# Decays over the whole unit, later weight loads, an apart first gate load and unit ends combined bank by bank, in a gated recurrence followed by an ELU MLP

## The chip, the cores and the metric

The kernel runs on one core of one Trainium2 chip. A core has five engines with a queue of their own each: TensorE (PE in the profile, with its weight loads as PEld), VectorE (DVE), ScalarE (ACT), GpSimd (POOL) and SyncE (SP), which here only starts DMA transfers. The metric is device time in microseconds (us). Nine runs of the kernel before gave a median of 586.71 us (585.16 to 588.66). The profile is one execution of its own: 586.64 us, of which the trace spans 584.9 us. PE, DVE, ACT and POOL each run their own list of instructions strictly in the order written, because the kernel turns the scheduler off.

## The reference

```python
batch, n_heads, seq, head_dim = (4, 8, 768, 48)
n_tokens, d_model, d_ff = (3072, 384, 2048)
...
    f = 1.0 / (1.0 + np.exp(-f_logit))
    for t in range(S):
        state = f[:, :, t, :, None] * state + np.einsum('bhd,bhe->bhde', k[:, :, t], v[:, :, t])
        y[:, :, t] = np.einsum('bhd,bhde->bhe', q[:, :, t], state)
...
    x = np.ascontiguousarray(attn_out.transpose(0, 2, 1, 3)).reshape(B * S, H * D)
    h = x @ w_in
    g = np.where(h > 0.0, h, alpha * (np.exp(np.minimum(h, 0.0)) - 1.0))
    return (g @ w_out).astype(np.float32)
```

Each of 32 heads carries a 48 by 48 state that decays per row with the gate f. The output x, 3072 tokens of 384 features, goes through a two-layer MLP with 2048 hidden units and ELU. q, k, v and f are float32, the two weights are float64 (eight bytes a number).

## The kernel before

**Units.** The tokens are cut into 12 units of 256 (`U`), three to a batch (`UPB`). Heads go in pairs `p` = 0 to 3 (`HP`): one head of a pair on partitions 0 to 47, the other on 64 to 111 (`HALF`), with padding rows between. A unit has four chunks of 64 tokens (`C`, `NC`).

**Attention of a unit.** `gates` (L556) turns f_logit into 1/f = 1 + exp(-x) on ACT (L563, L564). `decays` (L570) runs a cumulative product of 1/f along the tokens on DVE (L576), takes its reciprocal (L579), and scales k by the first (L580, POOL) and q by the second (L583). The product restarts at each chunk: POOL puts the first column of each chunk into the tile `restart` and zeros it in f (L566, L567), and the scan takes the maximum with `restart`. For pair 0 of unit 0 it restarts by being four scans of 64 columns instead. `watch` (L587) notes whether any product has passed `LIMIT` (the flag that sends the program to a slower general kernel). `transposed` (L593) transposes k on PE and copies it out on ACT (L602, tile `kn`); `advance` (L642) makes the states' increments; `step` (L606) runs the states from chunk to chunk on DVE: add (L613), times the chunk's decay (L616). `scores` (L619), `mask` (L635), `outputs` (L656) and `carried` (L675) give y. `carried` copies y into `xt` on ACT (L693, L695) and moves sixteen-row pieces of it with six small DMAs on SP (L699): piece i goes to column j = i mod 3, so that column j of `xt` is whole after pieces j and j + 3.

**MLP.** A step P is one unit m and one of eight blocks j of 256 hidden units. `up(P)` (L774) is 12 matmuls into `psH` (L780), with two passes on ACT (L785, L786); column kt of `xt` is used by the matmuls kt = 0, 1, 2 in turn. `elu(P)` (L789) finishes ELU on DVE (L792) and, for units from 2 on, makes four sums (L802). `down(P)` (L804) is 8 matmuls of 384 columns (L813, units 0 and 1) or, from unit 2 on, 7 products of half width with both weights and their combinations `combos` (L835, 14 matmuls), into four banks `pm[0]` to `pm[3]`; when a unit ends, ACT copies one half bank (L846) and five DVE additions (L845) make the output tile `o`, which four DMAs store (L854). Those of the last unit's second half go over ACT's queue, all others over SP's.

**Weights.** There are 16 items of 768 KB, half of them blocks of `w_in` (four DMAs each, L500 and L501), half of `w_out` (one DMA, L495). `fetch(n)` starts item n into one of seven slots of `area`. `split(n)` (DVE, L515, L519), `lower(n)` (ACT, L525) and `merge(n)` (DVE, L533) turn float64 into float32; `merge(n)` then starts `fetch(n + 7)` into the slot that it has emptied.

**Order.** The main loop runs T over two steps per P: `elu(P - 1)` and `up(P)` at even T, `down(P - 2)` at odd T. What else belongs to a step stands in `plan` under its T. `order` puts the first step of unit 1 (1, 0) at P = 6, T = 12. Before the loop the start runs unit 0's attention by hand (L886 to L926), with `warm(n)`, matmuls on the identity whose result is not used (L881). SP's queue before the loop holds, in this order: `load(0)` (f, k, q, v of unit 0; half of f, k and q on ACT's queue), `fetch(0)`, `load(1)`, `fetch(1)`, `fetch(7)` (from `merge(0)`), `fetch(2)` to `fetch(6)`. In the loop it goes on with `fetch(8)` to `fetch(11)`, `load(2)`, `fetch(12)`, `fetch(13)`, the six pieces of unit 1's `xt`, `fetch(14)`, `fetch(15)`, `load(3)`.

**Eight in flight.** The transfers of SP and ACT use eight completion semaphores in turn. So each issue waits until the transfer eight places before it has landed, whatever else it waits for.

Of the kernel before, what the change touches and what calls it, by code (L numbers as in the profile page):

```python
# [356 lines left out]
def fast(ctx: ExitStack, tc: tile.TileContext, q, k, v, f_logit, w_in, w_out, out, flag):  # L357
# [13 lines left out]

    nc = tc.nc
# [19 lines left out]
    LIMIT = 2.0**60  # L392
# [14 lines left out]
    def load(u, other=None):  # L407

        b, s0 = u // UPB, (u % UPB) * U
        for n in "fkq":  # L410
            for r in range(2):
                ((other or nc.sync) if r else nc.sync).dma_start(
                    out=qkf[u % NB][n][HALF[r]],
                    in_=src[n][b, r::2, :, s0 : s0 + U].rearrange("p d s -> d p s"),
                )
        nc.sync.dma_start(
            out=vs[u % NB][:, :, 0:DM], in_=v[b, s0 : s0 + U].rearrange("(c t) n -> t c n", t=W)
        )
# [13 lines left out]

    restart = cst.tile([128, HP, U], FP32, name="restart")
    nc.vector.memset(restart[:], 0.0)
    fine = cst.tile([128, HP, NC], FP32, name="fine")
# [120 lines left out]
    def gates(u, pieces=(2, 2)):  # L556

        f = qkf[u % NB]["f"]
        pts[u] = sb.tile([128, HP, U], FP32, tag="p", name=f"p{u}")
        p = 0  # L560
        for n in pieces:
            a = f[:, p : p + n]
            nc.scalar.activation(a, a, AF.Exp, scale=-1.0)  # L563
            nc.scalar.activation(a, a, AF.Copy, bias=1.0)  # L564
            if u or p:
                nc.gpsimd.tensor_copy(restart[:, p : p + n, ::C], a[:, :, ::C])  # L566
                nc.gpsimd.memset(a[:, :, ::C], 0.0)  # L567
            p += n

    def decays(u, p):  # L570
# [3 lines left out]
        for c in range(1 if u or p else NC):  # L574
            a = g if u or p else g[:, c * C : (c + 1) * C]
            nc.vector.tensor_tensor_scan(  # L576
                out=a, data0=a, data1=restart[:, p] if u or p else a, initial=1.0, op0=ALU.mult, op1=ALU.max
            )
# [8 lines left out]
    def watch(u):  # L587
        nc.vector.scalar_tensor_tensor(
            out=fine[:], in0=qkf[u % NB]["f"][:, :, C - 1 :: C], scalar=LIMIT, in1=fine[:],
            op0=ALU.is_le, op1=ALU.mult,  # L590
        )
# [14 lines left out]
    def step(u, c):  # L606
# [3 lines left out]
        now = pus[u][c % 2][:, c // 2]  # L610
        s = sb.tile([128, HP, D], FP32, tag="state", name=f"state{u}_{c}", bufs=5)
        if u % UPB or c:
            nc.vector.tensor_tensor(out=s[:], in0=now, in1=sts[u, c][:], op=ALU.add)  # L613
            now = s[:]
        decay = pts[u][:, :, (c + 1) * C - 1 : (c + 1) * C].broadcast_to([128, HP, D])
        nc.vector.tensor_tensor(out=s[:], in0=now, in1=decay, op=ALU.mult)  # L616
# [123 lines left out]
    plan, later = {}, {}  # L740

    def at_step(step, *todo):
        plan.setdefault(step, []).extend(todo)
# [60 lines left out]
    def down(P):  # L804
# [25 lines left out]
        for bank, half, x, y in (  # L830
            (0, 0, a[0][0], b[0][0]), (3, 0, a[0][1], b[1][0]), (0, 1, s[:, 1], c[1]),
            (1, 0, s[:, 0], c[0]), (1, 1, s[:, 2], c[2]), (2, 1, a[1][1], c[3]), (2, 0, s[:, 3], b[1][1]),
        ):
            first = j == 0 and (bank, half) in ((0, 0), (3, 0), (1, 0), (2, 1))
            nc.tensor.matmul(  # L835
                pm[bank][:, half * DH : (half + 1) * DH], lhsT=x, rhs=y,
                start=first, stop=(j == NP - 1), skip_group_check=True,
            )
        if j == NP - 1:
            p = [[pm[i][:, h * DH : (h + 1) * DH] for h in range(2)] for i in range(4)]  # L840
            o = sb.tile([128, 2, DM], FP32, tag="o", name=f"o{m}")
            u2 = sb.tile([128, DH], FP32, tag="u2", name=f"u2_{m}", bufs=1)
            u43 = sb.tile([128, 2, DH], FP32, tag="u43", name=f"u43_{m}", bufs=1)
            flat = o[:].rearrange("p t f -> p (t f)")
            add = lambda to, x, y: nc.vector.tensor_tensor(out=to, in0=x, in1=y, op=ALU.add)  # L845
            nc.scalar.copy(u2[:], p[0][0])  # L846
            add(flat[:, 0:DH], p[3][0], u2[:])
            add(u2[:], p[0][1], u2[:])
            add(u43[:], pm[1][:].rearrange("p (h f) -> p h f", h=2), u2[:].unsqueeze(1).broadcast_to([128, 2, DH]))
            add(flat[:, 3 * DH :], p[1][0], u43[:, 1])  # L850
            add(flat[:, DH : 3 * DH], pm[2][:], u43[:].rearrange("p h f -> p (h f)"))
            for t in range(2):
                for h in ((1, 0) if t else (0, 1)):
                    (nc.scalar if t and m == NU - 1 else nc.sync).dma_start(  # L854
                        out=out[m * U + t * 128 : m * U + (t + 1) * 128, h * DH : (h + 1) * DH],
                        in_=o[:, t, h * DH : (h + 1) * DH],
                    )
# [32 lines left out]
    fetch(1)  # L890
# [18 lines left out]
    for c in range(NC - 1):  # L909
# [3 lines left out]
        )  # L913

    if wide:
        nc.gpsimd.memset(area[:, 2:].bitcast(I32)[:, :, 0:1], 0)
    for n in range(2, AHEAD):
        fetch(n)
    split(1)
# [3 lines left out]
    lower(1)  # L923
    decays(1, 1)
    step(0, NC - 1)
    watch(0)  # L926
    blank(2, nc.gpsimd)
# [3 lines left out]
    attention(1, (), (2, 4, 5, 6, 7))  # L931
    for n in range(1, NFT):
        t = max(needs[n][0] - 2, 0)
        at_step(t, lambda n=n: merge(n))
        if n > 1:
            later.setdefault(max(t - 2, 0), []).append(n)
# [16 lines left out]
    for T in range(NU * NFT):  # L953
# [9 lines left out]
        for n in later.pop(T, ()):  # L963
            split(n)
            lower(n)
# [47 lines left out]
```

## Time and profile before

| what | value |
|---|---|
| median of 9 runs | 586.71 us |
| profiled execution, whole / span of its trace | 586.64 / 584.9 us |
| granted TensorE clock, mean | 0.992 of full |
| busy: PE, PEld, DVE, ACT, POOL | 566.8, 492.5, 398.2, 217.4, 78.9 us |
| moved by DMA in all | 50.81 MB |
| unit 0's first f load: issue, landing | 1.55 and 1.56, 4.0 and 4.3 us later |
| first ACT gate (L563) / first scan (L576) | 5.93 / 6.82 us |
| first issue of `load(1)` / of `fetch(1)` / of `fetch(7)` | 10.06 / 14.81 / 21.69 us |
| first psH matmul of P = 0 / P = 1 / P = 6 | 33.48 / 39.02 / 71.46 us |
| last psM matmul ends / last addition ends | 577.67 / 579.09 us |

A busy PE is one that has a matmul in its pipe; ends of matmuls are modelled. Busy times of the engines overlap and do not add up to the span. Times such as 71.46 us count from the span's start.

### The profile page before, as it was taken

Reading aid. Unit: us, or ns where it says so; the run is one execution under the profiler, and the core shown is the slowest. Engines: PE = TensorE matmul, PEld = TensorE weight load, DVE = VectorE, ACT = ScalarE, POOL = GpSimd, SP = SyncE. Lnnn points to the kernel's source line nnn. Section 1 sums busy time; section 2 is a strip of 40 time slices with the busy share of each in tenths; the row PEclk is TensorE's granted clock in tenths of the full one; section 3 lists DMA queues with packets and bytes.
Section 4 is the critical chain, followed back from the end, with each engine's and each line's share of the span. In section 5 each row is a group of like instructions: output and inputs, shape, how many; then the busy total and the mean of one; then the engine's idle time right before and its main releaser. Section 6 shows DMA issues by size and latency. Waiting matters only on the chain.

```text
span 584.9 us, 13417 instructions
## 1 busy us (share of the span) xinstructions
PE 566.8 (97%) x5596; PEld 492.5 (84%) x5596; DVE 398.2 (68%) x806; ACT 217.4 (37%) x357; POOL 78.9 (13%) x161
## 2 busy tenths in 40 slices
PE   7689999999999999999999999999999999999995
PEld 3467777777899999999999899899899999999994
DVE  7799667666586676576676776766766767665852
ACT  3367845433433332432423333243252252232221
POOL 6350021020020020020021011011011011000000
PEclk9889999999999999999999999999999999999999
DMA  8999880061071061052053043033024010305401
GB/s 183 239 235 270 184 196 0 2 124 47 2 156 40 3 126 69 4 93 88 19 85 92 21 83 91 27 66 105 29 52 118 29 54 10 136 17 208 136 3 33
DMA packets 34823, 50.81 MB, mean 87 GB/s; under 512 B 4000, under 2 KB 27584, under 8 KB 34752
## 3 DMA queue, kind: packets, MB, share of 16 engines
q1 hardware_dynamic: 33840, 49.07, 34.1%
q8 instruction: 46, 0.75, 0.6%
q10 hardware_dynamic: 912, 0.79, 0.6%
q14 instruction: 25, 0.20, 0.1%
HBM read 44.04 MB, written 4.72 MB: 83 GB/s over the span
## 4 chain that ended last, share of the span: by engine, by line
PE 92%; DMA 3%; ACT 1%; DVE 1%; POOL 1%; issue 0%; SPq 0%; DVEq 0%; POOLq 0%; ACTq 0%
PE psH L780 43%; PE psM L835 31%; PE psM L813 7%; PE psS L629 2%; PE psY L666 2%; PE psU_a L650 2%; PE psY L686 2%; PE psT L598 2%; DMA q<-in_q_dram 1%; DMA area<-in_moe_w_in_dram 1%; DMA f<-in_f_logit_dram 1%; PE psW L881 1%; ACT f L564 0%; ACT f L563 0%; ACT area L525 0%
## 5 line engine op out<-in xcount | busy, mean ns | idle before, releaser
L780 PE MATMUL psH<-xt,wi 128*128 128x256 f32 x1152 | 268.6, 383 | 0.0
L780 PEld LDWEIGHTS psH<-xt,wi 128*128 128x128 f32 x1152 | 213.7, 190 | 30.4 <-issue 0.5
L785 ACT ACTIVATE gg<-psH 128x512 f32<-128x512 f32 x96 | 57.3, 597 | 267.5 <-PE psH L780 267.3
L792 DVE SCALAR_TENSOR_TENSOR gg<-gg,psH 128x512 f32<-128x512 f32 x96 | 65.8, 685 | 109.0 <-ACT gg L786 109.0
L835 PE MATMUL psM<-area,sums 128*128 128x192 f32 x480 | 91.1, 326 | 0.0
L579 DVE RECIPROCAL p<-f 128x256 f32<-128x256 f32 x48 | 84.1, 1753 | 1.7
L835 PEld LDWEIGHTS psM<-area,sums 128*128 128x128 f32 x480 | 80.2, 190 | 0.0
L835 PE MATMUL psM<-wo,gg 128*128 128x192 f32 x320 | 65.2, 326 | 0.0
L786 ACT ACTIVATE gg<-gg 128x512 f32<-128x512 f32 x96 | 60.5, 630 | 3.0
L835 PEld LDWEIGHTS psM<-wo,gg 128*128 128x128 f32 x320 | 56.3, 190 | 4.0
L580 POOL TENSOR_TENSOR k<-k,f 128x256 f32<-128x256 f32 x48 | 35.5, 741 | 167.4 <-DVE f L576 157.7
L813 PE MATMUL psM<-wo,gg 128*128 128x384 f32 x128 | 44.2, 488 | 0.0
L802 DVE TENSOR_TENSOR sums<-gg 128x128 f32<-128x128 f32 x160 | 39.4, 288 | 2.8
L835 PE MATMUL psM<-area,gg 128*128 128x192 f32 x160 | 39.1, 326 | 0.0
L835 PE MATMUL psM<-wo,sums 128*128 128x192 f32 x160 | 39.1, 326 | 0.0
L845 DVE TENSOR_TENSOR o<-psM,u 128x192 f32<-128x192 f32 (+1 forms) x30 | 11.8, 420 | 38.4 <-ACT u L846 38.1
L566 POOL COPY restart<-f 128x8 f32<-128x8 f32 (+1 forms) x24 | 4.8, 200 | 243.2 <-ACT f L564 239.6
L813 PEld LDWEIGHTS psM<-wo,gg 128*128 128x128 f32 x128 | 24.1, 190 | 13.6
L525 ACT ACTIVATE area<-area 128x768 uint16<-128x768 uint32 x16 | 30.4, 1935 | 5.9 <-DVE area L519 5.8
L576 DVE TENSOR_TENSOR_SCAN f<-f,restart 128x256 f32<-128x256 f32 x47 | 32.0, 680 | 0.0
L551 DVE TENSOR_REDUCE spans<-area 128x1 f32<-128x768 f32 x32 | 28.9, 945 | 0.0
L835 PEld LDWEIGHTS psM<-area,gg 128*128 128x128 f32 x160 | 28.2, 190 | 0.0
(82 smaller groups left out, 461.7 us busy)
## 6 DMA issues: line engine op xcount, KB each, us to landing
area<-in_moe_w_out_dram SPq DMA_DIRECT2D x16, 768.0 KB, 7.1
area<-in_moe_w_in_dram SPq DMA_DIRECT2D x8, 768.0 KB, 6.9
v<-in_v_dram SPq DMA_DIRECT2D x12, 384.0 KB, 7.1
area<-in_moe_w_in_dram SPq DMA_DIRECT2D x16, 288.0 KB, 8.6
f<-in_f_logit_dram SPq DMA_DIRECT2D x23, 192.0 KB, 3.9
k<-in_k_dram SPq DMA_DIRECT2D x23, 192.0 KB, 5.1
q<-in_q_dram SPq DMA_DIRECT2D x23, 192.0 KB, 6.3
out_dram<-o SPq DMA_DIRECT2D x38, 96.0 KB, 1.7
```

Source lines behind the costliest of these rows:

```text
L525: nc.scalar.activation(raw.bitcast(U16)[:, 2::4], raw.bitcast(U32)[:, 0::2], AF.Copy, scale=2.0**-29)
L551: nc.vector.tensor_reduce(out=spans[:, i, n : n + 1], in_=area[:, 4 + n % (AHEAD - 4)].bitcast(FP32)[:, 1::2], axis=mybir.AxisListType.X, ...
L576: nc.vector.tensor_tensor_scan(out=a, data0=a, data1=restart[:, p] if u or p else a, initial=1.0, op0=ALU.mult, op1=ALU.max)
L579: nc.vector.reciprocal(pts[u][:, p], g)
L580: nc.gpsimd.tensor_tensor(out=t["k"][:, p], in0=t["k"][:, p], in1=g, op=ALU.mult)
L780: nc.tensor.matmul(ph[:, i], lhsT=wi[j][:, kt, i * 128 : (i + 1) * 128], rhs=xts[m][:, kt, :], start=(kt == 0), stop=(kt == NKT - 1),)
L785: nc.scalar.activation(g[:], ph[:], AF.Relu, scale=-1.0)
L786: nc.scalar.activation(g[:], g[:], AF.Exp, scale=-1.0)
L792: nc.vector.scalar_tensor_tensor(out=g[:], in0=g[:], scalar=-1.0, in1=phs.pop(P)[:], op0=ALU.add, op1=ALU.max)
L802: nc.vector.tensor_tensor(out=s[:, i], in0=x, in1=y, op=op)
L813: nc.tensor.matmul(pm[t][:], lhsT=g[:, i, t * 128 : (t + 1) * 128], rhs=wo[:, 2 * j + i, :], start=(j == 0 and i == 0), stop=(j == NP - 1 ...
L835: nc.tensor.matmul(pm[bank][:, half * DH : (half + 1) * DH], lhsT=x, rhs=y, start=first, stop=(j == NP - 1), skip_group_check=True,)
```

## The change

Seven edits come together. (1) `decays` runs the product over the whole unit of 256 tokens, with f itself as the second operand, so `restart` and POOL's two instructions per half unit go; `LIMIT` becomes 2^80, `fine` and `watch` look at the last column only, by two instructions of 48 partitions. (2) `step` no longer multiplies by a decay at each chunk; it does so once at the end of the unit, and the first chunk of a batch is a copy. (3) Unit 0's f is loaded as two pieces per half: pair 0 first, pairs 1 to 3 after it. (4) `fetch(1)` moves from before the start's work to after the first state of unit 0, together with `fetch(2)` to `fetch(6)`; SP's queue is then `fetch(0)`, `load(1)`, `fetch(7)`, `fetch(1)` to `fetch(6)`, and POOL's clearing of `area` moves up with it. (5) `split(1)` and `lower(1)` move behind unit 1's first two decays and unit 0's `watch`. (6) Unit 1's transposes come after `up(1)` instead of before it, and the later splits go through `plan` at half steps, which keeps their place. (7) The seven products of `down` come bank by bank (the second half of bank 2 goes to bank 3), the additions at a unit's end are issued as banks finish, there are six of them, each with its store behind it, and all stores are on SP's queue.

```diff
-    LIMIT = 2.0**60
+    LIMIT = 2.0**80
...
-        for n in "fkq":
+        for n, pairs in [("f", slice(0, 1)), ("f", slice(1, HP))] * (u == 0) + [("f", slice(0, HP))] * (u > 0) + [
+            ("k", slice(0, HP)), ("q", slice(0, HP))
+        ]:
             for r in range(2):
                 ((other or nc.sync) if r else nc.sync).dma_start(
-                    out=qkf[u % NB][n][HALF[r]],
-                    in_=src[n][b, r::2, :, s0 : s0 + U].rearrange("p d s -> d p s"),
+                    out=qkf[u % NB][n][HALF[r], pairs],
+                    in_=src[n][b, r::2, :, s0 : s0 + U].rearrange("p d s -> d p s")[:, pairs],
                 )
...
-    restart = cst.tile([128, HP, U], FP32, name="restart")
-    nc.vector.memset(restart[:], 0.0)
-    fine = cst.tile([128, HP, NC], FP32, name="fine")
+    fine = cst.tile([128, HP, 1], FP32, name="fine")
...
-            if u or p:
-                nc.gpsimd.tensor_copy(restart[:, p : p + n, ::C], a[:, :, ::C])
-                nc.gpsimd.memset(a[:, :, ::C], 0.0)
...
-        for c in range(1 if u or p else NC):
-            a = g if u or p else g[:, c * C : (c + 1) * C]
-            nc.vector.tensor_tensor_scan(
-                out=a, data0=a, data1=restart[:, p] if u or p else a, initial=1.0, op0=ALU.mult, op1=ALU.max
-            )
+        nc.vector.tensor_tensor_scan(out=g, data0=g, data1=g, initial=1.0, op0=ALU.mult, op1=ALU.max)
...
-        nc.vector.scalar_tensor_tensor(
-            out=fine[:], in0=qkf[u % NB]["f"][:, :, C - 1 :: C], scalar=LIMIT, in1=fine[:],
-            op0=ALU.is_le, op1=ALU.mult,
-        )
+        for rows in HALF:
+            nc.vector.scalar_tensor_tensor(
+                out=fine[rows], in0=qkf[u % NB]["f"][rows, :, U - 1 :], scalar=LIMIT, in1=fine[rows],
+                op0=ALU.is_le, op1=ALU.mult,
+            )
...
         if u % UPB or c:
-            nc.vector.tensor_tensor(out=s[:], in0=now, in1=sts[u, c][:], op=ALU.add)
-            now = s[:]
-        decay = pts[u][:, :, (c + 1) * C - 1 : (c + 1) * C].broadcast_to([128, HP, D])
-        nc.vector.tensor_tensor(out=s[:], in0=now, in1=decay, op=ALU.mult)
+            nc.vector.tensor_tensor(out=s[:], in0=new, in1=sts[u, c][:], op=ALU.add)
+        else:
+            nc.vector.tensor_copy(s[:], new)
+        if c == NC - 1:
+            end = pts[u][:, :, U - 1 :].broadcast_to([128, HP, D])
+            nc.vector.tensor_tensor(out=s[:], in0=s[:], in1=end, op=ALU.mult)
...
-            (0, 0, a[0][0], b[0][0]), (3, 0, a[0][1], b[1][0]), (0, 1, s[:, 1], c[1]),
-            (1, 0, s[:, 0], c[0]), (1, 1, s[:, 2], c[2]), (2, 1, a[1][1], c[3]), (2, 0, s[:, 3], b[1][1]),
...
-            nc.scalar.copy(u2[:], p[0][0])
-            add(flat[:, 0:DH], p[3][0], u2[:])
-            add(u2[:], p[0][1], u2[:])
-            add(u43[:], pm[1][:].rearrange("p (h f) -> p h f", h=2), u2[:].unsqueeze(1).broadcast_to([128, 2, DH]))
-            add(flat[:, 3 * DH :], p[1][0], u43[:, 1])
-            add(flat[:, DH : 3 * DH], pm[2][:], u43[:].rearrange("p h f -> p (h f)"))
-            for t in range(2):
-                for h in ((1, 0) if t else (0, 1)):
-                    (nc.scalar if t and m == NU - 1 else nc.sync).dma_start(
...
+            def put(t, h, x, y):
+                to = o[:, t, h * DH : (h + 1) * DH]
+                add(to, x, y)
+                nc.sync.dma_start(
+                    out=out[m * U + t * 128 : m * U + (t + 1) * 128, h * DH : (h + 1) * DH], in_=to
+                )
+
+            last = {
+                1: lambda: (nc.scalar.copy(u1[:], p[0][0]), add(u2[:], p[0][1], u1[:])),
+                3: lambda: (
+                    add(
+                        u43[:], pm[1][:].rearrange("p (h f) -> p h f", h=2),
+                        u2[:].unsqueeze(1).broadcast_to([128, 2, DH]),
+                    ),
+                    put(1, 1, p[1][0], u43[:, 1]),
+                ),
+                5: lambda: (put(0, 0, p[3][0], u1[:]), put(1, 0, p[3][1], u43[:, 1])),
+                6: lambda: put(0, 1, p[2][0], u43[:, 0]),
+            }
+        for n, (bank, half, x, y) in enumerate((
+            (0, 0, a[0][0], b[0][0]), (0, 1, s[:, 1], c[1]), (1, 0, s[:, 0], c[0]), (1, 1, s[:, 2], c[2]),
+            (3, 0, a[0][1], b[1][0]), (3, 1, a[1][1], c[3]), (2, 0, s[:, 3], b[1][1]),
+        )):
...
-    fetch(1)
...
+        if c == 0:
+
+            if wide:
+                nc.gpsimd.memset(area[:, 1:].bitcast(I32)[:, :, 0:1], 0)
+            for n in range(1, AHEAD):
+                fetch(n)
-
-    if wide:
-        nc.gpsimd.memset(area[:, 2:].bitcast(I32)[:, :, 0:1], 0)
-    for n in range(2, AHEAD):
-        fetch(n)
-    split(1)
     decays(1, 0)
     first_outputs(1)
     warm(2)
-    lower(1)
     decays(1, 1)
     step(0, NC - 1)
     watch(0)
+    split(1)
+    lower(1)
...
-    attention(1, (), (2, 4, 5, 6, 7))
+    attention(1, (), (2.5, 4, 5, 6, 7))
```

## The prediction

> **What bounds the kernel now.** I read the page first, then the chain of waits around the start, the stretches of five us, and SP's queue.
>
> ```profile
> PE 566.8 (97%) x5596; PEld 492.5 (84%) x5596; DVE 398.2 (68%) x806; ACT 217.4 (37%) x357; POOL 78.9 (13%) x161
> ...
> PEclk9889999999999999999999999999999999999999
> DMA  8999880061071061052053043033024010305401
> ```
>
> PE is busy for 97% of the span, but the DMA row has a second fact: its first six slices (14.6 us each) are full. So there are two candidates for the start, PE's chain and the stream of transfers. The chain of waits between 38 and 60 us:
>
> ```profile
> 37.96 0.74 POOL k L580
> ...
> 38.75 0.44 PE psT L598 x2
> 39.19 2.59 PE psH L780 x12
> 41.78 3.43 PE psW L881 x8
> ```
>
> The last work of another engine on PE's path is POOL's at 38.70. From there PE runs without a hole to its last matmul at 577.67. What comes later in the start is therefore passed on to the end, one for one, unless something else catches up with PE. Whether that can happen is told by SP's queue and unit 1's `xt`:
>
> ```profile
> L695 ACT COPY xt<-psY x2: 577/580/582, 61.0 to 61.6; 64x512 f32<-64x512 f32 x2
> ...
> 64.25 0.31 SPq L501 DMA_DIRECT2D area<-in_moe_w_in_dram  x1
> 65.76 4.49 SPq L699 DMA_DIRECT2D xt<-xt  x6
> ...
> xt<-xt SPq DMA_DIRECT2D x1, 16.0 KB, 1.8
> ...
> 71.46 2.75 PE L780 MATMUL psH<-xt,wi 128*128 128x256 f32 x12
> ```
>
> (The columns: start, length, engine, line; the fourth row is the sixth piece alone, issued at 69.67, with its time to landing.) `xt` of unit 1 is copied by 62.2, but its first piece is issued at 65.76: it stands behind `fetch(13)`, whose last part goes out at 64.25, and it waits for the transfer eight places before it, the first part of `fetch(12)`, issued at 57.37 and landing 8.3 us later, at 65.67. The sixth piece lands at 69.67 + 1.8 = 71.5. PE begins the first matmul that reads this `xt` at 71.46. So PE and the DMA stream reach P = 6 together.
>
> **The stream.** These are the transfers to be through before it:
>
> ```profile
> core 0: us, PE busy (x) PEld busy (x) DVE busy (x) ACT busy (x) POOL busy (x), PEclk, DMA share, GB/s
> ...
> 60.00:65.00 5.00, 5.00 (x21) 3.63 (x20) 2.30 (x4) 4.90 (x7) 0.00 (x0) 1.00 1.08 235
> 65.00:70.00 5.00, 5.00 (x21) 3.76 (x20) 3.53 (x7) 2.99 (x4) 0.00 (x0) 1.00 0.76 166
> ```
>
> From 5 to 65 us every stretch moves 200 to 336 GB/s at a share of 0.94 or more. The same bytes precede unit 1's `xt` after the change, in the same order but for `fetch(7)` going ahead of `fetch(1)`.
>
> **The change, part by part.**
>
> *PE's lead.* Pair 0's f comes as 2 x 48 KB. No row has that size at the start; a 16 KB piece lands in 1.8 us, the 192 KB f in 4.0 to 4.3. In proportion it would be 1.8 + 2.2 x 32/176 = 2.2; since two share the stream I take 2.6, so 4.2 instead of 5.86 (bounds 1.8 and 4.3). Two gates of 0.42 (L563, L564) follow, then four times scan and reciprocal, 0.68 + 1.75: DVE ends them near 14.8 instead of 16.54. POOL loses its two copies and two clears (0.20 and 0.11 each) and clears unit 1's tiles from 4.8 instead of 9.08; its first k product (11.77 now) then waits only for k's landing at 7.6. `merge(0)` hangs on this chain: it ends near 19.4 instead of 21.67. `fetch(7)` is issued there. SP waits at it with nothing else to send; behind it now stands `fetch(1)`, which needs a copy of 0.35 and POOL's 0.22 + 0.10 and goes out near 20.2 instead of 14.81. Two items of 768 KB at 225 to 339 GB/s (stretches between 20 and 27 us), about one us after issue, are through at 26 to 27 and landed by 28, against 17.66 + 8.1 = 25.8 now. DVE waits for that at `split(1)`, and behind it stand decays(1, 2) and (1, 3). But decays(1, 0) and (1, 1), which today come after it, now fill the wait (2.36 us of DVE idle before 25.93 today).
>
> From 27.3 on, DVE: 1.1 split(1), 2.4 decays(1, 2), 0.95 merge(1), 1.1 split(2), 2.4 decays(1, 3), 0.4 q, 0.3 watch, 1.1 split(3); then ACT: 1.95 lower(3), 1.25 gg, 1.2 kn. Together 14.2: unit 1's psU starts at 41.5 instead of 45.14. The transposes moved behind up(1) are ready by 38 (merge(1) 31.8, matmuls 2.8, k from POOL 35.3), hidden by ACT's list; without that cover they would cost their 1.04. So PE has a lead of 3.6 here, 2.5 if its first matmuls run on a low clock, 0 if `fetch(1)` lands after 31.
>
> *Two rules against it.* The 16 KB and 192 KB rows above leave 2.3 us to win by a small first piece. The Trainium skill, DMA: Bandwidth & Descriptors, section Rules for kernel authors, says that transfers under 64 KB are mostly overhead and should be joined. By that rule the f piece brings nothing and the sum below becomes 588.4; by the rows it stays 586.4. And PE's clock: PE stands for 4.36 us from 21.93, and the stretches 25 to 30 and 30 to 35 have a granted clock of 0.58 and 0.73; a stand of 1.86 us (36.89 to 38.75) shows no drop. The skill's TensorE: Matmul & The Clock Gate, section HAM oscillation — how this bites in real kernels, has no gap over about 3.4 us as its rule: by it a stand of 2 to 3 us before P = 6 costs only itself (586.4), by the longer row it could cost 3.4 more (589.8).
>
> *What catches the lead.* PE would want `xt` at 68 to 69. SP's list is unchanged there, and its xt issues wait for the landings of `fetch(12)` and `fetch(13)`. These shift only by what the stream loses or wins:
> - a hole after `load(1)`. Two loads and one item, 3.93 MB, are through at 20.0 to 20.4 (the stretches from 0 to 20 have 111, 239, 200 and 217 GB/s, 3.84 MB); `fetch(7)` issued at 19.4 flows about one us later. Loss 0 to 1.2; if `merge(0)` stayed at 21.67, 2.5. I take 0.5.
> - `fetch(11)` waits today for `merge(4)` (SP stands from 46.76 to 50.74), with only one item left in the queues; it goes out earlier. Win 0 to 0.5; I take 0.2.
>
> So the pieces land 0.3 later (-0.5 to +2.5). PE can start 0.5 earlier than now against them: the pair for kt = 0 is whole with the fourth piece (68.44 + 2.5 = 70.9), and the last column is used 4 x 0.216 = 0.86 after the start. Together 0.3 - 0.5 = -0.2 at P = 6 (-1.0 to +2.0), whatever PE's lead is between 0 and 3.5. That cover is needed: without the stream's limit the lead would go through to the end.
>
> *Steady part.* Off PE's path, so nothing: per unit DVE saves three products of 0.36 and adds one `watch` of 0.17, POOL saves 0.62. Today's cover is DVE's wait for ACT before L792 (109.0 us in all). Without it, a microsecond a unit would count, on the gain side. The products of `down` are the same 14 matmuls at 0.163 apart; both orders contain neighbours in one bank, and the timeline shows no wider step there. The unit end has six additions for five: they end at 186.98 now, about 0.4 later then, and the bank is wanted at 189.09; that cover gone, ten units would cost 4.
>
> *The end.* Additions end at 579.09. Then: the copy can start two products earlier (0.33), one addition of 0.36 more: last addition about as before. Four stores on one queue, each 0.35 to 0.48 of SP: the last issue at 579.2, as today's 579.12. Landing: the last three take 3.3 to 3.4 today, a lone one 1.6. A gain of 1.7 needs the landing to be the end; SP's own way to the end starts from its last issue. I take 0 (-1.7 to +0.3).
>
> **Sum.** 586.64 - 0.2 + 0 = 586.4, beside a median of 586.71: no change within 0.3% (1.76 us, what this kernel's runs can tell).
>
> **The rivals.**
> - *The lead survives* (faster). The stream runs faster than I think with deeper queues (w_out alone reached 336 GB/s in 50 to 55), so `xt` lands 2 to 3 earlier, or the store's landing was the end: 586.64 - 2.8 = 583.8. Against: twelve full stretches, with f, k, q and w_in never above 271. 0.25.
> - *The hole in the stream is the new bound* (slower). `merge(0)` hangs on psS, ACT's lower and POOL; if it slips to 21.7 or the drain of `load(1)` leaves engines idle, `fetch(1)` to `fetch(13)` all move by 2.5 to 3, and `xt` with them: 586.64 + 2.8 - 0.5 = 588.9. It decides from a hole of 2.3 on (1.8 + 0.5). A half clock after PE's wait at P = 6 would come on top: today's drop lost 5 x 0.42 + 5 x 0.27 = 3.4 us of clock. 0.18.
> - *It doesn't do what it says*: the products pass the limit and the general kernel runs. The inputs' largest product over a unit is 2^59, under 2^80: 0.01, inside the slower case.
>
> **How the numbers follow.** The forecast (same) has 0.57: its own range is 585.0 to 588.4. Faster by over 0.3% 0.25, slower 0.18. The range takes in both rivals' values: 583.6 to 589.0.
>
> **What would show it.** Right: `fetch(7)` issued at 19 to 20 and before `fetch(1)`; psU of unit 1 at 41 to 43; a wait of PE before psH of P = 6 with that matmul at 71 to 72 again, and xt issues at 65 to 67; from there the distance to the end unchanged. Wrong: P = 6 at 69 or earlier (the stream gave way), or a psH of P = 6 after 73; a PE hole at unit ends; an end that comes more than 0.5 earlier after the last addition.

## The result, and the profile after

The changed kernel is slower: a median of 592.59 us (589.06 to 594.86, 10 runs) against 586.92 us (31 runs of the kernel before), a ratio of 1.0086 with an interval of 1.0064 to 1.0107. Its profiled execution took 592.16 us, and the trace spans 590.4 us, 5.5 more than before. Medians here are of all runs; ratios leave disturbed runs out and are taken against the kernel before on the same chip, so kernels are compared by ratios.

From the page of the changed kernel (the last row: busy time, mean ns, then PE's idle time before these matmuls and what ended most of it):

```profile
PE 567.6 (96%) x5596; PEld 493.4 (84%) x5596; DVE 387.7 (66%) x792; ACT 217.8 (37%) x357; POOL 70.1 (12%) x113
...
PEclk9899989999999999999999999999999999999998
...
L777 PE MATMUL psH<-xt,wi 128*128 128x256 f32 x1152 | 270.2, 384 | 5.1 <-DMA xt<-xt 3.4
```

PE's work is the same (567.6 after 566.8 us). What is new is in the last row: PE waits 3.4 us for the transfers into `xt`. The order of time of PE shows where (start, length, then the work; in brackets the idle time ahead of it). The row below them is from the kernel before, whose P = 6 started at 71.46:

```profile
69.47 2.74 PE L810 MATMUL psM<-wo,gg 128*128 128x384 f32 x8
75.64 4.28 PE L777 MATMUL psH<-xt,wi 128*128 128x256 f32 x12 [3.42 <-DMA xt<-xt]
79.75 2.74 PE L810 MATMUL psM<-wo,gg 128*128 128x384 f32 x8
```

```profile
74.05 2.74 PE L813 MATMUL psM<-wo,gg 128*128 128x384 f32 x8
```

The middle row of the three is P = 6, which the prediction had at 71.46 again. PE could have begun it at 69.47 + 2.59 = 72.06, began at 75.64, and needed 79.75 - 75.64 = 4.11 until the next row instead of 2.59 (74.05 - 71.46 before). So the row behind P = 6 comes 5.70 later than before (79.75 against 74.05): 0.60 from PE's start, 3.58 of wait, 1.52 of slow matmuls. Stretches of five us (busy times of the engines, granted clock, DMA share, GB/s) show the slow part as a clock of 0.66:

```profile
core 0: us, PE busy (x) PEld busy (x) DVE busy (x) ACT busy (x) POOL busy (x), PEclk, DMA share, GB/s
10.00:15.00 5.00, 4.94 (x15) 2.18 (x14) 4.60 (x4) 0.59 (x1) 3.57 (x6) 1.00 1.09 166
...
20.00:25.00 5.00, 0.60 (x25) 0.60 (x28) 4.90 (x6) 0.86 (x2) 3.02 (x7) 0.90 1.07 298
25.00:30.00 5.00, 4.57 (x94) 3.50 (x87) 1.25 (x5) 1.35 (x5) 2.83 (x4) 0.50 1.06 186
...
70.00:75.00 5.00, 2.21 (x7) 0.95 (x5) 2.36 (x4) 4.90 (x7) 0.00 (x0) 1.00 0.53 125
75.00:80.00 5.00, 4.37 (x13) 3.64 (x14) 0.00 (x0) 0.05 (x1) 0.00 (x0) 0.66 0.77 250
```

and three of the same stretches in the kernel before:

```profile
10.00:15.00 5.00, 4.16 (x12) 1.73 (x12) 4.91 (x5) 0.58 (x1) 5.00 (x7) 1.00 1.09 200
...
20.00:25.00 5.00, 1.65 (x79) 1.26 (x72) 3.30 (x8) 2.88 (x5) 1.26 (x8) 1.00 1.07 225
25.00:30.00 5.00, 3.29 (x91) 2.90 (x94) 4.00 (x5) 0.33 (x2) 0.73 (x1) 0.58 1.06 271
```

The same rows show a second thing. From 10 to 15 us the DMA engines are as busy as before (a share of 1.09 both times) but move 166 GB/s instead of 200; from 25 to 30 it is 186 instead of 271. The first loss is made up by 25 us: until then the stretches of both kernels add up to 5.0 MB. From 25 to 50 us they add up to 5.2 MB after and 6.1 before, at shares of 1.04 and more. The stream is late without standing. SP's queue tells what that delays:

```profile
69.15 0.31 SPq L501 DMA_DIRECT2D area<-in_moe_w_in_dram  x1
70.43 4.58 SPq L696 DMA_DIRECT2D xt<-xt  x6
```

`xt` was copied by 62.7, but its first piece goes out at 70.43 (65.76 before), and the last lands at 76.26 (71.44 before). Going back along the landings, against the kernel before: `load(1)` +0.5, items 7 and 1 both there +2.6 (31.45), item 6 +3.6, item 11 +4.5, `load(2)` +4.9, `xt` +4.8.

At the start, PE's rows and DVE's:

```profile
24.40 1.11 PE L722 MATMUL psY<-at,padded_v 64*32 64x64 f32 x33 [4.56 <-issue]
...
35.98 2.83 PE L777 MATMUL psH<-xt,wi 128*128 128x256 f32 x12 [1.63 <-DVE wi L533]
...
44.81 0.31 PE L647 MATMUL psU_a<-v,kn 64*64 64x48 f32 x2 [1.70 <-ACT kn L597]
```

```profile
31.48 0.56 DVE L515 TENSOR_SCALAR bits<-area 128x768 int32<-128x768 int32 x1 [5.18 <-DMA area<-in_moe_w_in_dram]
```

DVE waits 5.18 us for item 1 at `split(1)`, so P = 1 waits (second row) and `kn` of unit 1 is late (third row): unit 1's psU begins at 44.81 against 45.14, so 0.33 is left of PE's lead, and by P = 6 (72.06 against 71.46) it is gone.

### The profile page after: what moved, and what is told of

Its sections match the earlier page's. It is cut to its first block, busy times and chain, and to the rows that moved or that the text cites. A ratio compares the mean times of both kernels' runs of the same rounds, so it can differ in the third digit from the quotient of the medians.

```text
span 590.4 us, 13417 instructions
## 1 busy us (share of the span) xinstructions
PE 567.6 (96%) x5596; PEld 493.4 (84%) x5596; DVE 387.7 (66%) x792; ACT 217.8 (37%) x357; POOL 70.1 (12%) x113
## 5 line engine op out<-in xcount | busy, mean ns | idle before, releaser
L861 PE MATMUL psM<-wo,gg 128*128 128x192 f32 x320 | 78.3, 326 | 0.0
L861 PEld LDWEIGHTS psM<-wo,gg 128*128 128x128 f32 x320 | 58.5, 190 | 4.0
L810 PEld LDWEIGHTS psM<-wo,gg 128*128 128x128 f32 x128 | 24.1, 190 | 13.6
L836 DVE TENSOR_TENSOR u<-psM,u 128x192 f32<-128x192 f32 (+1 forms) x20 | 9.2, 458 | 38.8 <-ACT u L846 37.8
L572 DVE TENSOR_TENSOR_SCAN f<-f 128x256 f32<-128x256 f32 x48 | 32.7, 682 | 1.1 <-ACT f L564 1.1
L861 PEld LDWEIGHTS psM<-wo,sums 128*128 128x128 f32 x160 | 28.2, 190 | 0.0
```

The lines of the kernel that those rows point to most:

```text
L572: nc.vector.tensor_tensor_scan(out=g, data0=g, data1=g, initial=1.0, op0=ALU.mult, op1=ALU.max)
L810: nc.tensor.matmul(pm[t][:], lhsT=g[:, i, t * 128 : (t + 1) * 128], rhs=wo[:, 2 * j + i, :], start=(j == 0 and i == 0), stop=(j == NP - 1 ...
L861: nc.tensor.matmul(pm[bank][:, half * DH : (half + 1) * DH], lhsT=x, rhs=y, start=(j == half == 0), stop=(j == NP - 1), skip_group_check=True,
```

## The experiments

Theories: **H**, the hole that the late item 1 opens in the stream makes `xt` late. **D**, the two more transfers of the split f shift the turn of the eight semaphores. **A**, the arithmetic (scan, additions, unit ends). After the first four runs came **S**: the change takes 4,128 bytes a partition out in front of `area`, so that its address changes, and transfers into it are slower.

All runs in one table. "Behind P = 6" is the start of the psM row after P = 6 in the trace; "rest" is the span less that.

| | kernel | median | ratio to before, interval | span | behind P = 6 | rest |
|---|---|---|---|---|---|---|
| | before | 586.92 | | 584.9 | 74.05 | 510.9 |
| | changed | 592.59 | 1.0086 (1.0064 to 1.0107) | 590.4 | 79.75 | 510.7 |
| E1 | changed, item 1 early | 591.50 | 1.0052 (1.0022 to 1.0082) | 589.9 | 78.97 | 510.9 |
| E2 | before, items late | 588.74 | 1.0039 (1.0021 to 1.0057) | 588.0 | 77.12 | 510.9 |
| E3 | before, f split | 588.06 | 1.0025 (1.0003 to 1.0047) | 587.2 | 76.39 | 510.8 |
| E4 | changed, xt first | 588.00 | 1.0030 (1.0007 to 1.0053) | 586.1 | 75.14 | 511.0 |
| E5 | changed, pad 32 | 590.48 | 1.0061 (1.0036 to 1.0086) | 588.8 | 77.97 | 510.8 |
| E6 | before, pad 32 | 588.97 | 1.0029 (1.0000 to 1.0057) | 588.8 | 78.33 | 510.5 |
| E7 | changed, pad 32, item 1 early | 587.23 | 1.0016 (0.9998 to 1.0035) | 584.4 | 73.65 | 510.8 |
| E8 | E7 and xt first | 585.29 | 0.9964 (0.9940 to 0.9989) | 583.7 | 72.80 | 510.9 |
| E9 | E8, pad ahead of f, q, k, v | 585.58 | 0.9967 (0.9941 to 0.9993) | 585.1 | 74.19 | 510.9 |
| E10 | E8, f whole | 585.44 | 0.9976 (0.9948 to 1.0003) | 581.9 | 71.10 | 510.8 |
| E11 | changed, pad 32, xt first | 587.62 | 1.0000 (0.9974 to 1.0026) | 587.0 | 76.23 | 510.8 |
| E12 | before, f split, xt first | 589.36 | 1.0028 (1.0002 to 1.0055) | 588.3 | 76.80 | 511.5 |
| E13 | changed, pad 64 | 593.52 | 1.0107 (1.0071 to 1.0142) | 590.7 | 79.38 | 511.3 |
| E14 | changed, 5 products in the wait | 593.32 | 1.0106 (1.0073 to 1.0140) | 591.6 | 80.81 | 510.8 |
| E15 | E8, transposes early | 585.06 | 0.9962 (0.9944 to 0.9981) | 583.4 | 72.34 | 511.1 |
| E16 | E12, transposes late | 588.80 | 1.0020 (0.9998 to 1.0042) | 586.9 | 76.22 | 510.7 |
| E17 | changed, 3 products in the wait | 591.77 | 1.0075 (1.0045 to 1.0104) | 589.3 | 78.39 | 510.9 |
| E18 | before, split(1) late, xt first | 586.39 | 0.9998 (0.9975 to 1.0020) | 584.3 | 72.91 | 511.4 |

The last column is the first finding. Over 20 traces whose spans go from 581.9 to 591.6, what follows P = 6 takes 510.5 to 511.5 us, with the old and with the new scan, products, `watch` and unit ends. So the loss arises before P = 6. That A costs nothing there either is shown further down: E15, which has all of it, is faster than E18, which has none.

**E1, item 1 back behind load(1).**

```diff
     load(1)
+    fetch(1)
...
-                nc.gpsimd.memset(area[:, 1:].bitcast(I32)[:, :, 0:1], 0)
-            for n in range(1, AHEAD):
+                nc.gpsimd.memset(area[:, 2:].bitcast(I32)[:, :, 0:1], 0)
+            for n in range(2, AHEAD):
```

> The changed kernel with item 1 fetched right after load(1) again (the other items after the first state, as in the change). Theory H (the hole after load(1), 2.1 us, and what follows from it makes unit 1's xt late): fetch(1) lands near 25.5 instead of 31.45, xt's last piece at 71 to 73 instead of 76.26, no wait of PE at P = 6 above 1 us, time 586 to 588. Theory D (the two more transfers of the split f shift the turn of the eight completion semaphores, and the drift of 2 us between 35 and 69 us comes from that): the stream still slips by 2 to 3, xt lands at 73.5 to 74.5, PE waits 1.5 to 2.5 at P = 6, time 588.5 to 590. Theory A (the arithmetic: additions, watch, unit ends): P = 6 has no part in it, time 592 to 593 again.

Item 1 landed at 29.06, but the stream was no faster: items 7 and 1 were both there at 32.34, `xt` at 76.85, later than in the changed kernel and than H (71 to 73) or D (73.5 to 74.5) had it. P = 6 waited 1.40 us. There was also no hole to be closed: in the changed kernel the DMA share is 0.95 or more in every microsecond from 18 to 26 us. H alone falls: there is another cause.

**E2 and E3, one part of the change alone in the kernel before.** E2 moves the fetches (and split(1), lower(1)) as the change does; E3 splits f.

```diff
-    fetch(1)
...
+        if c == 0:
...
+            for n in range(1, AHEAD):
+                fetch(n)
...
     watch(0)
+    split(1)
+    lower(1)
```

> The kernel before with the order of the fetches alone changed (item 1 after the first state, split(1) and lower(1) after watch(0)); f whole, old scan, old unit ends. Theory H: merge(0) stays at 21.7, so fetch(7) and fetch(1) go out 2 us later than in the changed kernel and the hole is 4 instead of 2.1: xt's last piece at 75 to 77.5, PE waits 3 to 6 at P = 6, time 591 to 594. Theory D: without the two more transfers no drift: the slip stays what the hole makes it, xt at 73.5 to 75.5, time 589 to 591.5. Theory A: 586 to 588.

E2 costs 0.39%, less than H forecast (588.74 for 591 to 594). Its DMA share from 20 to 25 us fell to 0.59: the hole, seen directly (the changed kernel has 1.07 there, above).

```profile
20.00:25.00 5.00, 2.83 (x135) 2.27 (x132) 4.71 (x9) 2.98 (x7) 2.31 (x9) 1.00 0.59 188
```

`xt` landed at 74.88, just ahead of H's 75 to 77.5 and inside D's range. In this trace PE reached P = 6 at 73.56, and waited 0.74 more, not 3 to 6.

```diff
-        for n in "fkq":
+        for n, pairs in [("f", slice(0, 1)), ("f", slice(1, HP))] * (u == 0) + [("f", slice(0, HP))] * (u > 0) + [
+            ("k", slice(0, HP)), ("q", slice(0, HP))
+        ]:
```

> The kernel before with unit 0's f alone split into pair 0 and the rest. Theory H: first gate at 3.7, the stream loses about 0.5 at the start (v0 and item 0 wait for semaphores two places later) and nothing after it; xt's last piece at 71.5 to 72.5; time 585 to 587.5. Theory D: the slip grows to 2 to 2.5 by 69 us, xt lands at 73.5 to 74.5 and PE waits about 2 at P = 6: 588 to 590. Theory A: 586.5 to 587.

E3 gains nothing, and loses 0.25% (0.03 to 0.47). The first gate was early as forecast, but PE left its stand at psY<-at,padded_v at 26.44 (26.28 before), although it came there 1.3 earlier, and P = 1 ran on a low clock (4.32 instead of 2.75 us). `xt` landed at 74.39 and the time is 588.06, both as D forecast, and H's 71.5 to 72.5 for `xt` was missed. But PE came to P = 6 at 73.80 and didn't wait there, so the wait that D forecast isn't shown. E7 and E10 below come back to D.

**E4, unit 1's xt ahead of items 12 and 13.**

```diff
-        fetch(n + AHEAD)
+        if n not in (5, 6):
+            fetch(n + AHEAD)
...
+    at_step(7, lambda: fetch(12), lambda: fetch(13))
     at_step(12, lambda: gates(2))
```

> The changed kernel with items 12 and 13 issued behind unit 1's xt pieces instead of ahead of them (items needed at steps 16 and 20). Theories H and D alike: the stream is as late as in the changed kernel, but the xt pieces no longer wait for items 12 and 13; they follow load(2) and land at 67 to 71; no wait at P = 6, no half clock in 75 to 80 us, time 586 to 588. Theory A: 592 to 593, as the wait was only hiding something that ends as late. A rival of its own: the pieces queue behind load(2)'s 1.3 MB of 1 KB packets and land after 73 still, time 589 to 591.

`xt` landed at 68.66, no wait at P = 6, no low clock there: 0.56% (0.25 to 0.87) less than the changed kernel, though the stream was as slow. So the wait at P = 6 is where the late stream becomes time.

**E5 to E7, the address of area.** Packets in the traces gave the hint: after E4, those of 2,048 bytes took 152 to 164 ns in the three kernels with the old tiles in front of `area`, 167 to 183 in the three with the new ones. An unused tile of 32 bytes moves `area`, and nothing else changes.

```diff
+    cst.tile([128, 8], FP32, name="pad")
     fine = cst.tile([128, HP, 1], FP32, name="fine")
```

> The changed kernel with one unused tile of 32 bytes a partition ahead of fine. Nothing but addresses moves: the change took 4,096 + 32 bytes out in front of the fetch area (its base 120,320 before, 116,192 after: 32 past a multiple of 64); with the pad it is a multiple of 64 again. In the first 100 us a packet of 2,048 bytes took 155 ns in the kernel before, 167 in the changed one. Theory S (the address of the area slows the transfers into it): 2,048-byte packets at 152 to 158 ns, the stream 2 us earlier at f13, PE's wait at P = 6 from 3.4 to about 1, time 588.5 to 590.5. Theory H (the hole after load(1) and what follows is all): packets 160 to 185 ns whatever the address, time 591.5 to 593.5. Theory D (turn of the semaphores): as H.

The same line in the kernel before (E6), where it takes the good address away:

```diff
+    cst.tile([128, 8], FP32, name="pad")
     fine = cst.tile([128, HP, NC], FP32, name="fine")
```

> The kernel before with the same unused tile of 32 bytes: the area's base goes from 120,320 to 120,352, 32 past a multiple of 64; nothing else changes. Theory S: 2,048-byte packets at 165 to 180 ns instead of 155, xt of unit 1 lands 2 to 4 later, PE waits at P = 6, time 588 to 590.5. Theories H and D: 586 to 587.5, packets at 152 to 158 ns.

And in E1 (E7):

```diff
+    cst.tile([128, 8], FP32, name="pad")
...
     load(1)
+    fetch(1)
...
```

> The first experiment (changed kernel, item 1 right after load(1)) with the 32-byte tile. Theory S: the stream is as fast as before and has no hole; 2,048-byte packets at 152 to 158 ns, f13 lands at 70 to 71.5, xt at 71.5 to 73, time 585.5 to 588, so 3.5 to 5 less than the first experiment's 591.5. Theories H and D: no difference to it, 590 to 592.5.

Times went as S says in all three pairs: 0.25% from the changed kernel to E5, 0.36% from E1 to E7, 0.29% from E6 to the kernel before. Together 0.30% with an interval of 0.11 to 0.49, so 0.6 to 2.9 us. (In E5 the mean of the 2,048-byte packets, 167 ns, is a miss: it changes with the load. So is the wait at P = 6, 3.00 instead of about 1.) E4 and E11 below, which differ by the pad alone, make a fourth pair with the same 0.30%. PE's rows of E5, then of E7:

```profile
22.60 1.12 PE L723 MATMUL psY<-at,padded_v 64*32 64x64 f32 x33 [1.82 <-issue]
...
35.45 4.51 PE L778 MATMUL psH<-xt,wi 128*128 128x256 f32 x12 [2.77 <-DVE wi L534]
...
73.62 4.51 PE L778 MATMUL psH<-xt,wi 128*128 128x256 f32 x12 [3.00 <-DMA xt<-xt]
```

```profile
26.11 1.12 PE L723 MATMUL psY<-at,padded_v 64*32 64x64 f32 x33 [5.38 <-issue]
...
70.98 2.83 PE L778 MATMUL psH<-xt,wi 128*128 128x256 f32 x12 [0.62 <-DMA xt<-xt]
```

The two differ in item 1's place alone. With it late (E5), P = 1 and P = 6 both wait and then run on a low clock; with it early (E7), `xt` is there at 71.70 instead of 74.44 and the wait is 0.62. That is 0.45% of time. With the changed kernel less E1 (0.34%) and E2 (0.39%), the place of item 1 costs 0.39% on average (0.22 to 0.56), so 1.3 to 3.3 us, beside S. (E2 moves `split(1)` too; E8 and E11 below, which differ by item 1's place alone, give 0.36%.) With both taken back, E7's ratio is 1.0016 (0.9998 to 1.0035): of the change's 0.86% the two account for 0.70% (0.42 to 0.98), and what is left isn't clear of noise. E7's f is split too, and its `xt` landed only 0.3 later than in the kernel before (71.44), so D isn't needed for the lateness.

**E13, the control of the pad.** A tile of 64 bytes moves everything as well, but leaves `area` off the boundary.

```diff
+    cst.tile([128, 16], FP32, name="pad")
```

> The changed kernel with an unused tile of 64 bytes instead of 32: the area's base is 116,256, still 32 past a multiple of 64. Theory S: as the changed kernel, 591.5 to 593.5, and less than a third of the 3,072-byte packets at exactly 121 ns (23 to 30% in the four kernels with the area 32 past, 42 to 70% in the others). The theory that any move of the tiles does it: 589.5 to 591, more than 42%.

593.52 us: a tile as such does nothing. (Each pad moves the tiles behind it too, not `area` alone; that the transfers into `area` are what changes rests on the packets.) What counts shows in packets that nothing disturbs, which take the same time over and over (shares of all packets of that size, counted in the traces):

| base of area past a multiple of 256 | kernels | 3,072 bytes at just 121 ns, first 100 us | 6,144 bytes at just 234 ns, later | 2,048 bytes, mean ns |
|---|---|---|---|---|
| 0 | before, E2, E3, E5, E7 to E12, E15, E16, E18 | 42 to 70% | 76 to 82% | 152 to 179, mean 165 |
| 32 | E6, E13 | 27, 33% | 47, 48% | 171, 178 |
| 224 | changed, E1, E4, E14, E17 | 23 to 36% | 47 to 48% | 167 to 183, mean 176 |

The second most frequent times off the boundary are 125 and 238 ns. Every base here that is a multiple of 64 is one of 256 too, so the runs don't tell these apart. The Trainium skill, DMA: Bandwidth & Descriptors, section How a descriptor splits into AXI transactions, says that an AXI transaction, of at most 256 bytes, must start at a multiple of 256. It says so of reads; here it is the written side that moved. An estimate from that: a packet of 3,072 bytes off the boundary would take 13 transactions instead of 12. The sign agrees; but by the page's count of beats a start at 224 would waste far more than one at 32, and the two lower rows are alike. Why about half of the packets keep the short time isn't known.

How the two causes meet shows in the bytes that the engines moved between 25 and 50 us, counted in the traces:

| | `area` on the boundary | `area` off it |
|---|---|---|
| item 1 early | 5.6 to 6.3 MB (before, E3, E7 to E10, E12, E15, E16, E18) | 5.2, 5.0 MB (E1, E6) |
| item 1 late | 5.2 to 5.5 MB (E2, E5, E11) | 4.8 to 5.3 MB (changed, E4, E13, E14, E17) |

Either of the two alone slows the stream, and both together hardly more. A hole goes with the late item 1 only in E2 and E5 (DMA shares of 0.59 and 0.72 from 20 to 25 us); in the other six kernels that have item 1 late the share is 0.96 to 1.08. So the place of item 1 costs, but not by the hole that H named; why the busy stream moves less with item 1 late stays open.

**E8 to E11, what is left.** E8 is E7 with xt first:

```diff
-        fetch(n + AHEAD)
+        if n not in (5, 6):
+            fetch(n + AHEAD)
...
+    at_step(7, lambda: fetch(12), lambda: fetch(13))
```

> The last one with items 12 and 13 issued behind unit 1's xt pieces as well. Theory S with H: xt lands by 66 to 68, PE keeps what lead it has at psU of unit 1 (1 to 3 us), time 583.5 to 586. Theory D or H alone: the stream stays slow, but xt no longer hangs on it: 586.5 to 588.5, as the kernel with xt first and nothing else (588.0).

E9 moves its pad:

```diff
+    cst.tile([128, 8], FP32, name="pad")
     qkf = [{n: cst.tile([128, HP, U], FP32, name=f"{n}{i}") for n in "fqk"} for i in range(NB)]
```

> The eighth experiment (pad, item 1 early, xt first; 585.3) with the 32-byte tile put ahead of f, q, k and v instead of ahead of fine: now these 32-past tiles lie on multiples of 64 too, the area as there. Theory S for every transfer: packets of 1,024 bytes at 70 to 76 ns instead of 80 to 82 in the first 100 us, load(1) through 1 to 2 earlier, time 583.5 to 585. Theory S for the area alone (or for 2 and 3 KB packets alone): 80 to 82 ns again, 585 to 586.

E8 is faster than the kernel before by 0.36% (0.11 to 0.60). E9 brings f, q, k and v to multiples of 64 (not of 256) and changes nothing: 1,024-byte packets took 84 ns. E10 is E8 with f whole, E11 is E8 with item 1 late:

```diff
-        for n, pairs in [("f", slice(0, 1)), ("f", slice(1, HP))] * (u == 0) + [("f", slice(0, HP))] * (u > 0) + [
...
+        for n in "fkq":
...
```

> The eighth experiment with unit 0's f whole again. The theory that the split f gives PE nothing, since PE leaves its stand at psY<-at,padded_v at 25.5 to 26.6 in every kernel with item 1 early, whether it arrives at 19.8 or at 21.9 (the 16 KB instruction transfer starts at 22.7 to 23.7 there): 585 to 586, no difference. The theory that the lead of the split f is worth something: 586.5 to 587.5. Theory D (its two transfers shift the turn of the semaphores and cost): 583.5 to 584.5.

```diff
     load(1)
-    fetch(1)
...
-            for n in range(2, AHEAD):
+            for n in range(1, AHEAD):
```

> The changed kernel with the pad and with xt ahead of items 12 and 13, but item 1 still late. Theory H and S: the stream is as late as in the padded kernel (590.5), but nothing at P = 6 waits for it; what remains of the late item 1 is PE's wait for merge(1) at P = 1 (2.8 in the padded kernel) less the earlier end of the stand at psY<-at,padded_v (22.6 instead of 26): 585 to 587. A theory that the late item 1 costs beyond P = 6 (fetch(11) to f15 later): 587.5 to 589.

E10: no difference to E8 (0.12%, within 0.37), so neither the lead of the split f nor D can be shown (PE left its stand at 24.41 here, a miss). In its trace `xt` landed 2.3 earlier than in E8, as it did 3.0 earlier in the kernel before than in E3, so D isn't excluded; the two pairs differ in time by 0.07% on average (-0.15 to 0.28). E11: 0.36% (0 to 0.72) more than E8, and 587.62 is above the 585 to 587 of H and S, though its rest (510.8) shows no cost beyond P = 6; with no wait at P = 6 left, the late item 1 costs at P = 1 (1.19), at `kn` (1.73) and by a low clock behind that (psH of 4.49 at 47.41).

**E12, E15, E16, E18, DVE's order.** E12 is the kernel before with E3's edit and E4's:

```diff
+        for n, pairs in [("f", slice(0, 1)), ("f", slice(1, HP))] * (u == 0) + [("f", slice(0, HP))] * (u > 0) + [
...
+        if n not in (5, 6):
+            fetch(n + AHEAD)
...
+    at_step(7, lambda: fetch(12), lambda: fetch(13))
```

> The kernel before (area on a multiple of 64, item 1 early as it was) with the split f and xt first: the eighth experiment without the new scan, watch, products and unit ends. Theory A' (the arithmetic is worth nothing either way): 584.5 to 586, as the eighth. Theory that POOL's clears and copies of the old scan hold up the start: 586 to 587.5. Theory that the new unit ends or watch cost something: 583 to 584.5.

E15 is E8 with unit 1's transposes ahead of up(1) again, E16 is E12 with them behind it.

```diff
-    attention(1, (), (2.5, 4, 5, 6, 7))
+    attention(1, (), (2, 4, 5, 6, 7))
```

> The eighth experiment (585.3) with unit 1's transposes ahead of up(1) again. Theory T (the transposes' place: PE waits there for POOL's k and cannot begin P = 1): a wait of 2 to 4 before psT, then half clock, 587.5 to 590. Theory POOL (its copies and clears made k late; they are gone here): k in time, 585 to 586.5.

```diff
-    attention(1, (), (2, 4, 5, 6, 7))
+    attention(1, (), (2.5, 4, 5, 6, 7))
...
+        for f in plan.pop(T + 0.5, ()):
+            f()
         for n in later.pop(T, ()):
```

> The twelfth experiment (kernel before with split f and xt first, 589.4) with unit 1's transposes behind up(1), nothing else. Theory T: 585 to 586.5, no wait ahead of P = 1. Theory POOL: k is late all the same and psU of unit 1 waits for it, 588 to 589.5.

E12 met none of its forecasts. PE's and DVE's rows of E12:

```profile
40.16 0.69 PE L601 MATMUL psT<-ident,k 128*128 128x128 f32 x2 [3.38 <-POOL k L583]
```

```profile
27.34 0.56 DVE L517 TENSOR_SCALAR bits<-area 128x768 int32<-128x768 int32 x1 [5.34 <-DMA area<-in_moe_w_in_dram]
...
28.41 0.68 DVE L579 TENSOR_TENSOR_SCAN f<-f,restart 128x256 f32<-128x256 f32 x1
```

and DVE's of E15:

```profile
20.77 0.68 DVE L574 TENSOR_TENSOR_SCAN f<-f 128x256 f32<-128x256 f32 x1
...
28.15 0.56 DVE L516 TENSOR_SCALAR bits<-area 128x768 int32<-128x768 int32 x1 [1.74 <-DMA area<-in_moe_w_in_dram]
```

E15 and E16 speak against the transposes' place, and POOL's list in E16 against its own copies, though both times lie in the range of the theory POOL: POOL stood 6.92 us for DVE's f there. In E12 unit 1's first scan stands behind `split(1)` and its wait for item 1; in E15 it runs 7 us ahead of it. E18 makes that exchange in the kernel before, with xt first (its f is whole, where E12 and E16 split it):

```diff
-    split(1)
     decays(1, 0)
     first_outputs(1)
     warm(2)
-    lower(1)
     decays(1, 1)
     step(0, NC - 1)
     watch(0)
+    split(1)
+    lower(1)
```

> The kernel before with two edits of order and nothing else: split(1) and lower(1) behind watch(0), items 12 and 13 behind unit 1's xt. Theory V (DVE's order in the start is what the changed kernel gains by; scan, products, split f and unit ends bring nothing): unit 1's first decays fill DVE's wait for item 1, no wait of PE for POOL's k above 1 us, 584.5 to 586. Theory that the new arithmetic has a part in it: 586.5 to 588. As the kernel before: 586.5 to 587.2, if its start is bound by something else.

PE's wait for POOL's k is gone in E18's trace, and the row behind P = 6 comes at 72.91 instead of 76.80. The times point the same way, without settling it: 0.26% (-0.03 to 0.55) less than E12 and E16 on average, a difference that E18's whole f could make as well. V's 584.5 to 586 was missed (586.39, a ratio of 0.9998). E15 is another 0.36% (0.06 to 0.66) below E18; which of scan, products, split f and POOL's lighter list that is stays open.

**E14 and E17, the low clock behind P = 6.**

```diff
+    at_step(12, lambda: warm(5), lambda: gates(2))
```

> The changed kernel with five 512-column products of the identity (2.1 us at full clock) put ahead of P = 6, into PE's wait for xt; their result is not used. Theory that the half clock after the wait costs on top (4.28 instead of 2.75 for psH of P = 6): 590.5 to 591.5, psH of P = 6 at 2.75 to 2.85. Theory that the wait costs only itself: 592 to 593.

The size in this expectation was wrong: the five products took 4.46 us, longer than the wait, and made PE late. E17 has three:

```diff
+    at_step(12, lambda: warm(3), lambda: gates(2))
```

> The changed kernel with three 512-column products in PE's wait at P = 6 (ten records took 4.46 us for five, so 2.7 for three). Theory that the half clock after the wait costs on top: psH of P = 6 at 2.75 to 2.85, 590.8 to 591.8, so about 1.5 less than the changed kernel (592.6). Theory that the wait costs only itself, or that other waits of the run decide: 592 to 593.5.

```profile
72.85 2.74 PE L891 MATMUL psW<-ident 128*128 128x512 f32 x6
75.69 2.87 PE L777 MATMUL psH<-xt,wi 128*128 128x256 f32 x12
```

P = 6 begins at 75.69, as in the changed kernel (75.64), and takes 2.87 instead of 4.28, at a clock of 1.00 (75 to 80 us, where the changed kernel has 0.66): the low clock comes from the wait and costs 1.4 in the trace. The time (0.11% less, within 0.36) can't show it by itself.

**The best version** is E15 (585.06) or E8 (585.29), which the runs don't tell apart: the change with `area` on the boundary, item 1 early and unit 1's `xt` ahead of items 12 and 13.

## Why the prediction was wrong

- *"From there PE runs without a hole; what comes later in the start is passed on, unless something else catches up."* Right, and so were *steady part 0* and *the end 0*: the rest is 510.7 us after and 510.9 before. From the last addition to the end it is 6.0 us against 5.8.
- *PE and the stream meet at P = 6.* Right, and the sign that was named for "wrong", a psH of P = 6 after 73, came: 75.64.
- *The step that failed: "the pieces land 0.3 later (-0.5 to +2.5)".* They landed 4.8 later. Two terms of it. All that item 1's place could cost the stream was a hole, taken as 0.5. The changed kernel has no hole, but the place cost 1.3 to 3.3 us by the pairs. And the working said "the same bytes", in the same order but for `fetch(7)`, and took their speed as unchanged: the address of `area`, 0.6 to 2.9 us, wasn't in it. The diff showed it: `restart` goes and `fine` shrinks, ahead of the tile that the stream fills. The 0.2 to be won at `fetch(11)` wasn't there; it landed 4.5 later.
- *Pair 0's f in 2.6 us, so at 4.2.* Too cautious: 1.87 and 2.10 us, at 3.4 and 3.6; the first gate came at 3.68. `merge(0)` ended at 19.62 (19.4 forecast), `fetch(1)` went out at 20.31 (20.2). All of this was near enough and worth nothing measurable (E3, E10). The missing row: PE's stand at psY<-at,padded_v, 4.36 us in the chain before, which the prediction used only for the clock. With item 1 early PE left it at 24.4 to 27.1, whenever it came.
- *Item 1 landed by 28, psU of unit 1 at 41.5, 0 lead if it lands after 31.* It landed at 31.45, and psU came at 44.81. The bound was right, the value taken not.
- *decays(1, 0) and (1, 1) fill DVE's wait.* They ran in it; E12, E16 and E18 bear it out in their traces. But item 1 came so late that DVE still stood 5.18 us.
- *Of the two rules of the Trainium skill*, the one on small transfers (DMA: Bandwidth & Descriptors, Rules for kernel authors) doesn't decide when the first consumer waits for the landing: 1.87 and 2.10 us for 48 KB against 4.0 and 4.3 for 192 KB, with the rest of f there at 5.4 and 5.7, no later than the whole f before (5.6 and 5.8). The one on PE's clock fits this wait: 3.42 us brought a low clock. It cost 1.5, not the 3.4 of the earlier row. That a stand of 2 to 3 us costs only itself fails in E5, where 3.00 us at P = 6 brought one too (4.51).
- *The rivals.* "The hole in the stream is the new bound" had the place right, P = 6 waiting for `xt`, and the way there only in part: `merge(0)` came early enough and no engine was idle, yet the late item 1 cost. Its 588.9 lacked the address; the low clock was named as coming on top, and came. "The lead survives" would have needed what E8 changes.

## What to carry to other kernels

A tile removed ahead of a DMA target is a change of the target's address: compare bases before the arithmetic. Where two chains meet, as PE and the stream do at P = 6, look what stands in the queue ahead of the transfer that the meeting waits for; here two items that are needed four and eight steps later stood in front of 0.1 MB. An instruction that waits for a late transfer belongs behind the work that doesn't need it.

## What the runs showed of the hardware

- *PE's own instructions come through the busy DMA engines.* The profile of the changed kernel counts a DMA queue of the kind "instruction" (q8: 46 packets, 0.75 MB). In all 20 traces PE's stand in `first_outputs` ends 1.3 to 1.6 us after one of its 16 KB transfers, and that it waits for it is inferred from this alone: 23.47 to 24.95 before (PE goes on at 26.28), 21.84 to 22.94 in the changed kernel (24.40), 20.20 to 21.30 in E5 (22.60). Stands of 1.4 to 2.1 us without any other releaser appear again at psS of unit 1 in E6, E13, E14 and E17.
- *The clock has no fixed length of gap.* A low clock came at P = 1 or behind after gaps of 1.73 (E11), 1.91 (E3), 2.30 (E4), 2.57 (E1) and 2.77 us (E5), none after 1.99 (E13) and 2.11 (E17). The Trainium skill, TensorE: Matmul & The Clock Gate, section HAM oscillation — how this bites in real kernels, has no gaps over about 3.4 us as its rule; these gaps are shorter.
- *A few microseconds of the start vary from run to run*: twelve runs of E1 go from 585.66 to 594.71, twelve of E15 from 583.84 to 586.00.
